# Hash attention and a PReLU feed-forward block on one core: w_out's groups moved to GpSimd's DMA queue and a block later, one step of each weight piece moved behind a reciprocal, second-product weights asked for sooner

## Chip, cores and metric

The kernel runs on one core of a Trainium2 chip. The metric is device time in microseconds (us) of one execution; a kernel's time is the median over its runs. The core has TensorE (PE, matrix products), VectorE (DVE), ScalarE (ACT), GpSimd (POOL) and SyncE (SP), which here only issues DMAs. Each of SP, ACT and POOL has a DMA queue of its own: what an engine issues goes out in the engine's program order, and an issue that has to wait holds up every later one on that engine.

## What is computed

Cut from the reference:

```python
# q, k, v: (4, 8, 768, 64); proj: (64, 6)
q_bucket = sum((q @ proj > 0) * 2 ** arange(6)); k_bucket likewise
scores = where(q_bucket == k_bucket, q @ k.T / 8, -1e9)
attn_out = softmax(scores) @ v
x = attn_out.transpose(0, 2, 1, 3).reshape(3072, 512)
# w_in: (512, 2048), w_out: (2048, 512), alpha: (2048,)
h = x @ w_in
g = maximum(h, 0) + alpha * minimum(h, 0)
out = g @ w_out
```

## The kernel before

`fast_path` does the work in float32. (Another path, `general_path`, stands behind a flag computed at run time and is not entered with these inputs.)

**Attention.** There are 16 pairs (batch, two heads) and two query halves of 384, so 32 units u. For each unit PE computes the scores of six key blocks (L729), ACT takes the exponentials (L734), and PE multiplies them with v (`attend`, L762) into one PSUM bank, tag "av", which has one buffer. The row sums come from DVE and from one accumulating DMA on POOL's queue (L743 to L752: `accp` and `accd`), and PE totals them (`totals`, L774). `divide` (from L778) turns the totals into reciprocals and multiplies: a DVE transpose `st` (L792), two small steps and the reciprocal `rr` (L794), four small POOL copies between partition groups (L797, L798), a DVE transpose `dn` (L800), and L803, which reads the bank "av" and writes x. x goes to a DRAM buffer `x_s` (L804).

**Weight pieces.** Beside the attention, the kernel rewrites the 32 pieces (128x512) of w_in and w_out, one piece a unit: load on SP (L567), `weight_abs` on ACT (L580), `weight_parts` on DVE (four steps, L587 to L592; the first, L587, clamps the piece and keeps its maximum), then `weight_sum` (L613, L618). `divide` calls its argument `between` after the POOL copies have been issued and before `dn`; from unit 1 on this is `weight_rest`, that is `weight_sum(u)` and `weight_group(u)`. So DVE has two weight steps to do while POOL copies. Groups of finished pieces are stored to DRAM, as `w_in_s` and `w_out_r`. `keep_in_program_order` (`do`) fixes the order of the compute instructions on each engine as written; DMA issues outside `do` are placed by the scheduler, by when their buffers come free.

**The two products.** After the attention come, for each of four batches, 8 blocks "1" (`ff1`, x times a weight group, names f_0 to f_7) and 7 blocks "2" (`ff2`, names z_1, z_2, z_5, z_6, z_3, z_7, z_4). Each block is a product of 2x2 blocks done with seven block products instead of eight (L849). Its steps in PE's order are 2 (bank b), 5 (c), 6 (a), 3 (c), 7 (a), then step 1 of the next block (bank a), then step 4 (a). The banks b and c have one buffer each. DVE combines the parts: for f blocks `finish` (L891, L895) four times, and after the "21" part four differences (L899). I call these finish 11, 12, 22 and 21. For z blocks DVE also makes sums of weights (`ws`, L959) and of g (`gs`, L967) for the next block. Between these, DVE runs `sum_out(n)` (L941, four operations 128x256) for the groups n = 0 to 7 of w_out: it takes a group loaded from `w_out_r` (L934), forms sums in place, and the result is stored to `w_out_s` (L942).

**Buffers and loads around the change.** The weight group of an f block, `wi`, is 896 KB with two buffers: `load_w(j + 2)` (L828) can go only when block j's last matmul has read its group. The tag "wl" has two buffers too, and serves w_out's groups (`wo`: tiles of two groups, so wo0, wo2, wo4, wo6) and then the second product's weights (`wl`, 1024 KB, L923). `load_out(n + 3)` follows each odd `sum_out(n)`. All these DMAs are on SP's queue. In SP's order before the change they alternate: wo0, wo2, store 0, wi2, store 1, wi3, wo4, wi4, and so on. `largest` and `verdict` (in block 4) compute the flag on DVE, with four transposes on PE (L1051).

Of the kernel before, what the change touches and what calls it, by code (L numbers as in the profile page):

```python
# [12 lines left out]
ALU = mybir.AluOpType  # L13
# [393 lines left out]
def fast_path(  # L407
# [12 lines left out]
    nc = tc.nc  # L420
# [18 lines left out]
    HI_MIN = 2.0 ** -15  # L439
    HI_END = 2.0  # L440

    do = tc.keep_in_program_order
    PE, DVE, ACT, POOL = nc.tensor, nc.vector, nc.scalar, nc.gpsimd
# [24 lines left out]
    NI = NF // 2  # L468
    NM = 7
    w_in_s = dram.tile([NI, P, NM, 2, P], F32, name="w_in_s")  # L470
    w_out_r = dram.tile([4, P, NI, DM // 2], F32, name="w_out_r")
    w_out_s = dram.tile([4, P, NI, DM // 2], F32, name="w_out_s")
# [90 lines left out]
    def load_weight(i):  # L563
        if i < NW:
            i = order[i]
            raw[i] = pool.tile([P, 512], moe_w_in.dtype, name=f"raw{i}", tag="raw", bufs=3)
            nc.sync.dma_start(raw[i], piece(i))  # L567
# [8 lines left out]
    def weight_abs(i):  # L576
        i = order[i]
        lo, hi = halves(i)
        wx[i] = pool.tile([P, 512], F32, name=f"wx{i}", tag="wx")
        do(ACT.activation(wx[i], hi.bitcast(F32), AF.Abs))  # L580

    def weight_parts(i):
        i = order[i]
        lo, hi = halves(i)
        x = wx[i]
        wr[i] = r = pool.tile([P, 512], F32, name=f"wr{i}", tag="wr", bufs=1)
        do(DVE.tensor_scalar(x, x, HI_MIN, None, op0=ALU.max, op1=ALU.max, accum_out=wmax[:, i : i + 1]))  # L587
        do(DVE.tensor_scalar(
            x.bitcast(U32), x.bitcast(U32), 3, 0xC0000000, op0=ALU.logical_shift_left, op1=ALU.bitwise_xor,
        ))  # L590
        do(DVE.tensor_scalar(r.bitcast(U32), x.bitcast(U32), 0x7F800000, None, op0=ALU.bitwise_and))
        do(DVE.scalar_tensor_tensor(r, lo, 2.0 ** -52, r, op0=ALU.mult, op1=ALU.mult))  # L592
# [31 lines left out]
    def weight_group(i):  # L624

        i = order[i]
        if i >= HW:
            n, m = divmod(i - HW, 2)
            if m == 1:
                nc.sync.dma_start(w_out_r[:, :, n].rearrange("m p d -> p m d"), wst[HW + n])  # L630
            return
        n, m = divmod(i, 4)
        if m < 3:
            return
        w = wst[n]

        def one(to, a, op, c):
            do(DVE.tensor_tensor(w[:, to], w[:, a], w[:, c], op=op))

        def store():  # L640
            c, kk = divmod(n, 2)
            for ii in range(4):
                nc.sync.dma_start(w_in_s[4 * c + ii][:, :, kk], w[:, :, ii])


        for x in ((3, 5, 2), (5, 0, 5), (4, 3, 0), (6, 1, 4)):
            sums_due.append((one, (x[0], x[1], ALU.subtract, x[2])))
        sums_due.append((store, ()))
# [129 lines left out]
    def divide(u, between=lambda: None):  # L778

        pi, g = divmod(u, NCH)
        b, hp = pairs[pi]
        if g == 0:
            vsum[pi] = pool.tile([P, 1], F32, name=f"vs{pi}", tag="vs")
            do(DVE.tensor_scalar(vsum[pi], av[u][:, CW : CW + 1], EPS, None, op0=ALU.mult))
        n = HW2 // 32
        a = pool.tile([P, HW2], F32, name=f"st{u}", tag="st", bufs=1)
        r = pool.tile([P, n], F32, name=f"rc{u}", tag="rc")
        rr = pool.tile([P, 2, n], F32, name=f"rr{u}", tag="rr")  # L790
        d = pool.tile([P, CW], F32, name=f"dn{u}", tag="dn", bufs=1)
        do(DVE.transpose(a, sums[u]))  # L792
        do(DVE.tensor_scalar(r, a.rearrange("p (n w) -> p n w", w=32)[:, :, 0], S * EPS, None, op0=ALU.add))
        do(DVE.reciprocal(rr, r.unsqueeze(1).to_broadcast([P, 2, n])))  # L794
        for q0 in (0, D):
            q1 = q0 + 32
            do(POOL.tensor_copy(rr[q0 : q0 + 32, 1], rr[q1 : q1 + 32, 1]))  # L797
            do(POOL.tensor_copy(rr[q1 : q1 + 32, 0], rr[q0 : q0 + 32, 0]))  # L798
        between()
        do(DVE.transpose(d, rr.rearrange("p h n -> p (h n)").unsqueeze(2).to_broadcast([P, 2 * n, 32])))  # L800

        x = mid.tile([P, CW], F32, name=f"x{u}", tag="x")
        do(DVE.scalar_tensor_tensor(x, av[u][:, :CW], vsum[pi], d, op0=ALU.add, op1=ALU.mult))  # L803
        nc.sync.dma_start(x_s[b, hp][:, g * CW : (g + 1) * CW], x)  # L804
# [124 lines left out]
    def load_out(n):  # L929

        if n < NI:
            t = late[0].tile([P, 2, 4, DM // 2], F32, name=f"wo{n}", tag="wl")
            for i in range(2):
                nc.sync.dma_start(t[:, i], w_out_r[:, :, n + i].rearrange("m p d -> p m d"))  # L934
                w_o[n + i] = t[:, i]

    def sum_out(n):

        w = w_o[n]
        for to, x, op, y in ((2, 3, ALU.add, 2), (3, 0, ALU.subtract, 3), (0, 2, ALU.subtract, 0), (1, 1, ALU.subtract, 0)):  # L940
            do(DVE.tensor_tensor(w[:, to], w[:, x], w[:, y], op=op))  # L941
        nc.sync.dma_start(w_out_s[:, :, n].rearrange("m p d -> p m d"), w)  # L942
        if n % 2:
            load_out(n + 3)

# [143 lines left out]
    add_first(0)  # L1089
    hash_bits(0, second)  # L1090
    weight_abs(0)
    weight_parts(0)
    weight_sum(0)
    for name in "qk":
# [2 lines left out]
    for u in range(UNITS):  # L1097
        pi, g = divmod(u, NCH)

        def weight_rest():  # L1100
            weight_sum(u)
            weight_group(u)

        scores(u, 1)
        if u < last:
            scores(u + 1, 0)
        if u:
            divide(u - 1, weight_rest)
        load_weight(u + 3)
        add_last(u)  # L1110
        add_total(u)
        if u < last:
            add_first(u + 1)
        else:
            now = ff1(0, 0)
            now.step(1)
            now.step(5)
        if g == 0 and pi + 1 < NPAIR:
            hash_bits(pi + 1)
        if g == 1 and pi + 2 < NPAIR:  # L1120
            turn(pi + 2, "q")
            turn(pi + 2, "k")
        if u < last:
            weight_parts(u + 1)
        weight_sums(1)
        attend(u)
        totals(u)
        if u == last:
            divide(u)
        if g == 1 and pi + 2 < NPAIR:  # L1130
            load(pi + 2, "v")
        if u == HW + 2:
            load_w(0)
            load_w(1)
            load_x(0)
        if HW + 4 <= u < HW + 8:
            sum_x(0, u - HW - 4, DVE)
        if u + 2 < NW:
            weight_abs(u + 2)
        if u == 1:  # L1140
            setup_alpha()
        if g == 1:
            for name in "qk":
                magnitude(pi, name)
                if pi + 3 < NPAIR:
                    load(pi + 3, name)
# [10 lines left out]
    for j, (b, what, n) in enumerate(blocks):  # L1157
        n2 = n + 1 if what == "2" else 0 if n == NI - 1 else 7
        if n2 == 0:
            sides_g(b, 0)  # L1160
            sum_w2(b, 0, 3, 4)
        now.step(2) if j else now.step(6)
        if j == 0:
            now.step(3)
            now.step(7)
            now.step(2)
        now.step(22)
        if j == 4:
            largest()
        if 0 < n2 < 7:  # L1170
            sides_g(b, n2)
            sum_w2(b, n2, 3, 4)
        if n2 < 7:
            sum_g2(b, n2, 3, 4)
        if j:
            now.step(5)
            now.step(6)
            now.step(3)
            sum_w2(b, n2, 6)
            now.step(7)  # L1180
            sum_w2(b, n2, 5)
            sum_g2(b, n2, 5)
        if j == 4:
            verdict()
        for n_out in [(0,), (1,), (2,), (3, 4), (5,), (6,), (7,)][j] if j < 7 else ():
            sum_out(n_out)
        if what == "1":
            load_w(b * NI + n + 2)
            if n >= NI - 2:
                load_w2(b, n - NI + 2)  # L1190
        else:
            load_w2(b, n + 2)
            if b + 1 < B:
                if n == 0:
                    load_x(b + 1)
                if n == 6:
                    for m in range(4):
                        sum_x(b + 1, m, DVE)
        if j + 1 < len(blocks):
            turn_out()  # L1200
        else:
            turn_last(0)
        before = now
        if j + 1 < len(blocks):
            b1, what1, n1 = blocks[j + 1]
            now = ff1(b1, n1) if what1 == "1" else ff2(b1, n1)
            now.step(1)
        before.step(4)
        if n2 < 7:
            sum_g2(b, n2, 6)  # L1210
# [29 lines left out]
```

## Time and profile before

| | |
|---|---|
| median of 6 runs | 910.84 us (908.12 to 912.0) |
| the profiled execution, whole time | 913.6 us |
| its span, first to last instruction | 911.8 us |
| mean granted TensorE clock | 0.995 |
| busy: PE / DVE / ACT / POOL | 890.0 / 757.4 / 408.6 / 88.3 us |
| attention and first f_0 steps | 0 to about 353 us |
| first f blocks (f_0 to f_7) | about 353 to 430 us |
| bytes moved | 146.88 MB, mean 161 GB/s |
| transfers on POOL's queue (q0) | 12.58 MB, all of them accp |

The profile is of one execution. "Busy" is the time in which an engine had an instruction in work; PE's busy time says nothing of how well it is used, but its idle time is time in which no matmul ran. A list of waits names, for each group of instructions, whom it waited for, how long in all, how many times, and the longest. A timeline line has start, duration, engine, line of the kernel, operation, what is written from what is read, the shapes, and, in square brackets, the idle time before it and what ended it. "SPq" and "POOLq" are the issues of DMAs on the engines' queues; "to landing" is the time from issue until the data is there.

### The profile page before, as it was taken

What the parts mean: (1) busy time and instruction counts of PE and PEld (TensorE: products, weight loads), DVE (VectorE), ACT (ScalarE), POOL (GpSimd) and SP (SyncE); (2) the same over time, 40 slices, a digit from 0 to 9 for tenths busy, and PEclk for the clock granted to TensorE, in tenths of its full rate; (3) what the DMA queues carried; (4) which work ended last, traced back from release to release, by engine and by line L of the source; (5) the groups of instructions that cost most, each with busy time, mean ns of one, the idle gap of its engine ahead of it and who ended that gap; (6) DMA issues with size and microseconds to landing.
All of it is one profiled execution on the core that took longest, in us unless ns stands there. A gap on an engine that the chain in (4) does not pass through costs nothing.

```text
span 911.8 us, 15639 instructions
## 1 busy us (share of the span) xinstructions
PE 890.0 (98%) x5885; PEld 591.5 (65%) x5885; DVE 757.4 (83%) x1353; ACT 408.6 (45%) x733; POOL 88.3 (10%) x178
## 2 busy tenths in 40 slices
PE   8999999999999999899999999999999999999996
PEld 4444454444444445556998556998556998556996
DVE  4888988988998997798989677989768989768985
ACT  7888888877878873222111222111222111222111
POOL 1222222222223221000000000000000000000000
PEclk9999999999999999999999999999999999999998
DMA  8787887699688764667433535333525242521242
GB/s 225 190 199 163 214 227 187 171 262 244 164 209 204 181 176 150 207 226 246 176 116 110 160 117 162 122 120 109 171 105 174 109 139 88 177 99 40 93 142 70
DMA packets 138053, 146.88 MB, mean 161 GB/s; under 512 B 78304, under 2 KB 126192, under 8 KB 134384
## 3 DMA queue, kind: packets, MB, share of 16 engines
q1 hardware_dynamic: 127248, 132.42, 46.9%
q0 software_dynamic: 8704, 12.58, 8.5%
q8 instruction: 48, 0.79, 0.4%
q10 hardware_dynamic: 2016, 0.79, 0.3%
q14 instruction: 37, 0.30, 0.1%
HBM read 104.87 MB, written 28.31 MB: 146 GB/s over the span
## 4 chain that ended last, share of the span: by engine, by line
PE 56%; DMA 3%; DVE 2%; SPq 1%; issue 1%; POOL 0%; ACT 0%; ACTq 0%; DVEq 0%; POOLq 0%
DMA wi<-w_in_s 3%; PE f_2a L849 2%; PE f_7a L849 2%; PE z_3a L849 2%; PE z_6a L849 2%; PE z_1a L849 2%; PE z_2a L849 2%; PE z_7a L849 2%; PE z_5a L849 2%; PE z_4a L849 2%; PE f_3a L849 2%; PE f_6a L849 2%; PE f_5a L849 2%; PE f_4a L849 2%; PE f_1a L849 2%; PE f_0a L849 2%
## 5 line engine op out<-in xcount | busy, mean ns | idle before, releaser
L734 ACT ACTIVATE pt<-sc 128x768 f32<-128x768 f32 x192 | 152.7, 813 | 53.9 <-PE sc L729 51.3
L729 PE MATMUL sc<-qT,kT 64*128 64x384 f32 x768 | 155.3, 482 | 0.0
L762 PE MATMUL av<-pt,vn 128*32 128x384 f32 (+1 forms) x1536 | 130.6, 488 | 4.9 <-DVE x L803 4.8
L762 PEld LDWEIGHTS av<-pt,vn 128*32 128x32 f32 x1536 | 46.6, 109 | 80.9 <-issue 66.1
L729 PEld LDWEIGHTS sc<-qT,kT 64*128 64x128 f32 x768 | 68.2, 188 | 35.0 <-issue 34.8
L899 DVE TENSOR_TENSOR g<-g,g 128x384 f32<-128x384 f32 x128 | 68.4, 555 | 2.2
L729 PE MATMUL sc<-qb,kb 64*128 64x384 bf16 x384 | 63.4, 324 | 1.9 <-ACT kb L717 1.0
L744 POOL DMA_DIRECT2D accp<-pt x32 | 38.5, 1204 | 193.8 <-issue 93.4
L967 DVE TENSOR_TENSOR gs<-g,gs 128x768 f32<-128x768 f32 x56 | 53.4, 953 | 1.0
L959 DVE TENSOR_TENSOR ws<-wl 128x512 f32<-128x512 f32 x56 | 38.6, 689 | 18.2 <-DMA wl<-w_out_s 15.9
L967 DVE TENSOR_TENSOR gs<-g 128x768 f32<-128x768 f32 x56 | 53.4, 953 | 0.0
L895 DVE SCALAR_TENSOR_TENSOR g<-h,alpha 128x384 f32<-128x384 f32 x32 | 19.8, 617 | 30.3 <-ACT h L888 30.3
L729 PEld LDWEIGHTS <-kb 64*128 64x128 bf16 x384 | 19.4, 94 | 33.2 <-issue 11.1
L752 DVE TENSOR_TENSOR accd<-accd,accp 128x768 f32<-128x768 f32 x32 | 30.7, 958 | 7.7 <-DMA accp<-pt 6.7
L706 ACT ACTIVATE qb<-hs,hb 32x384 bf16<-32x384 f32 x62 | 35.5, 573 | 1.1
L749 DVE TENSOR_TENSOR accd<-accd,pt 128x768 f32<-128x768 f32 x32 | 30.7, 959 | 3.3
L800 DVE STREAM_TRANSPOSE dn<-rr 128x384 f32<-128x384 f32 x32 | 18.5, 579 | 17.4 <-POOL rr L798 17.4
L743 DVE TENSOR_TENSOR accp<-pt,pt 128x768 f32<-128x768 f32 x32 | 30.5, 952 | 2.6 <-ACT pt L734 2.6
L748 DVE TENSOR_TENSOR accd<-pt,pt 128x768 f32<-128x768 f32 x32 | 30.4, 949 | 0.0
L798 POOL COPY rr<-rr 32x6 f32<-32x6 f32 x64 | 27.6, 431 | 2.6
L979 DVE TENSOR_TENSOR m<-m,m 128x768 f32<-128x768 f32 (+1 forms) x36 | 27.1, 752 | 0.7
L717 ACT ACTIVATE kb<-hs,hb 64x384 bf16<-64x384 f32 (+1 forms) x47 | 27.1, 577 | 0.6
(334 smaller groups left out, 1797.3 us busy)
## 6 DMA issues: line engine op xcount, KB each, us to landing
wi<-w_in_s SPq DMA_DIRECT2D x32, 896.0 KB, 4.8
wl<-w_out_s SPq DMA_DIRECT2D x16, 1024.0 KB, 4.8
accp<-pt POOLq DMA_DIRECT2D x32, 384.0 KB, 5.5
wl<-w_out_r SPq DMA_DIRECT2D x12, 1024.0 KB, 4.9
raw<-in_moe_w_out_dram SPq DMA_DIRECT2D x16, 512.0 KB, 5.1
raw<-in_moe_w_in_dram SPq DMA_DIRECT2D x16, 512.0 KB, 4.4
w_in_s<-wsi SPq DMA_DIRECT2D x16, 448.0 KB, 5.7
vn<-in_v_dram SPq DMA_DIRECT2D x16, 384.0 KB, 5.9
```

What stands on the lines that cost most here:

```text
L706: do(ACT.activation(bits["q", pi][D * s : D * s + 32, cols], ps["q"][c : c + 32, half, :CW], AF.Sign, bias=hb[c : c + 32],))
L729: do(PE.matmul(sc[:, s, :CW], what["k", pi][r, ks], what["q", pi][r, qs], start=first, stop=not first,))
L734: do(ACT.activation(pt[:, :, :CW], sc[:, :, :CW], AF.Exp, scale=SCALE / DOWN))
L743: do(DVE.tensor_tensor(accp[u], p(u, 0), p(u, 1), op=ALU.add))
L744: nc.gpsimd.dma_start(accp[u], p(u, 2), accum_op=ALU.add)
L749: do(DVE.tensor_tensor(accd[u], accd[u], p(u, 5), op=ALU.add))
L752: do(DVE.tensor_tensor(accd[u], accd[u], accp[u], op=ALU.add))
L762: do(PE.matmul(av[u][D * s + t : D * s + t + 32, :w], nat["v", pi][:, s, kc * D + t : kc * D + t + 32], prob[u, kc][:, s, :w], start=(kc = ...
L849: do(PE.matmul(self.ps[bank], self.left(left, k), self.right(right, k), start=start and k == 0, stop=k == self.nk - 1, skip_group_check=no ...
L899: do(DVE.tensor_tensor(new_g(b, to)[:, i], g_m[b, x][:, i], g_m[b, y][:, i], op=ALU.subtract))
L959: do(DVE.tensor_tensor(t, w2[b, n, x], w2[b, n, y], op=op))
L967: do(DVE.tensor_tensor(t, g2[b, n, x], g2[b, n, y], op=ALU.subtract))
```

## The change

Three edits:

1. The clamp (L587) is taken out of `weight_parts` into a function of its own, and is called for piece u + 1 in `weight_rest` of unit u, after `weight_sum` and `weight_group`, that is between the POOL copies and `dn`. For the first two pieces it is called ahead.
2. `load_out` and `sum_out` issue their DMAs on POOL's queue instead of SP's, and the groups are summed a block later: none in block 0, then 0, 1, 2, (3, 4), 5, (6, 7) in blocks 1 to 6; before it was 0, 1, 2, (3, 4), 5, 6, 7 in blocks 0 to 6.
3. For batches 1 to 3, `load_w2(b, 0)` and `load_w2(b, 1)` are called in the f blocks 4 and 5 instead of 6 and 7. For batch 0 the condition is the same as before.

```diff
+    def weight_clamp(i):
+        if i < NW:
+            i = order[i]
+            x = wx[i]
+            do(DVE.tensor_scalar(x, x, HI_MIN, None, op0=ALU.max, op1=ALU.max, accum_out=wmax[:, i : i + 1]))
+
     def weight_parts(i):
...
-        do(DVE.tensor_scalar(x, x, HI_MIN, None, op0=ALU.max, op1=ALU.max, accum_out=wmax[:, i : i + 1]))
...
-                nc.sync.dma_start(t[:, i], w_out_r[:, :, n + i].rearrange("m p d -> p m d"))
+                nc.gpsimd.dma_start(t[:, i], w_out_r[:, :, n + i].rearrange("m p d -> p m d"))
...
-        nc.sync.dma_start(w_out_s[:, :, n].rearrange("m p d -> p m d"), w)
+        nc.gpsimd.dma_start(w_out_s[:, :, n].rearrange("m p d -> p m d"), w)
...
     weight_abs(0)
+    weight_clamp(0)
     weight_parts(0)
...
             weight_sum(u)
             weight_group(u)
+            weight_clamp(u + 1)
...
             divide(u - 1, weight_rest)
+        else:
+            weight_clamp(1)
...
-        for n_out in [(0,), (1,), (2,), (3, 4), (5,), (6,), (7,)][j] if j < 7 else ():
+        for n_out in [(), (0,), (1,), (2,), (3, 4), (5,), (6, 7)][j] if j < 7 else ():
             sum_out(n_out)
         if what == "1":
             load_w(b * NI + n + 2)
-            if n >= NI - 2:
-                load_w2(b, n - NI + 2)
+
+            if 0 <= n - NI + (4 if b else 2) < 2:
+                load_w2(b, n - NI + (4 if b else 2))
```

## Prediction

> **What bounds the kernel now.** The page's first part has TensorE (PE) busy 890.0 us of a span of 911.8, so only 21.8 us can be won without taking matmuls away, and the order of PE's and ScalarE's instructions is the same in both kernels. I therefore read the list of waits for PE first, then PE's timeline around each wait, then the timelines of what released it: VectorE (DVE) and SyncE's DMA queue (SP). In the list (engine, tile and line waited for: us in all, times, longest):
>
> ```profile
> PE av L762 <- DVE x L803: 4.8, 9, 1.2
> PE f_2a L849 <- DMA wi<-w_in_s: 2.5, 2, 2.3
> PE sm L774 <- DVE accd L752: 1.4, 1, 1.4
> ...
> PE f_7a L849 <- DMA wi<-w_in_s: 1.1, 1, 1.1
> ...
> PE f_6a L849 <- DMA wi<-w_in_s: 0.5, 1, 0.5
> ```
>
> Two stages hold them. In the attention, the bank "av" has one buffer, so attend(u) waits until DVE's L803 has read it for unit u-1: nine waits, seven of them after 230 us. At the start of the first product, PE waits for weight groups (wi). The rest are start-up and tail, which the change does not touch. Here is PE's timeline where block 1 passes to block 2, and the windows table over the same time (a stretch, its length, busy us of PE, PE's weight loads, DVE, ScalarE and POOL, then granted clock, DMA share, GB/s):
>
> ```profile
> 366.23 1.45 PE L849 MATMUL f_1a<-x,wi 128*128 128x384 f32 x4
> 370.01 2.21 PE L849 MATMUL f_2a<-x,wi 128*128 128x384 f32 x4 [2.33 <-DMA wi<-w_in_s]
> 372.01 2.54 PE L849 MATMUL f_1a<-x,wi 128*128 128x384 f32 x4
> 374.39 1.45 PE L849 MATMUL f_2b<-x,wi 128*128 128x384 f32 x4
> ...
> 368.00:372.00 4.00, 1.99 (x4) 1.13 (x5) 2.86 (x7) 0.25 (x1) 0.00 (x0) 0.85 0.13 56
> 372.00:376.00 4.00, 4.00 (x10) 2.29 (x9) 0.90 (x2) 0.96 (x2) 0.00 (x0) 0.73 0.54 147
> ```
>
> Undisturbed steps start 1.29 us apart. These three intervals take 374.39 - 366.23 = 8.16 instead of 3.87: 4.29 us lost, of which 370.01 - 367.52 = 2.49 is late data and 1.80 the clock, granted at 0.85 and 0.73. By the same sum the passage to block 6 (407.45 to 412.13) loses 0.81 and to block 7 (417.29 to 422.50) 1.34, both at clock 1.00. Together **6.44 us**. Why the group was late stands in SP's timeline:
>
> ```profile
> 357.29 2.02 SPq L934 DMA_DIRECT2D wo<-w_out_r  x4
> 363.22 0.36 SPq L942 DMA_DIRECT2D w_out_s<-wo  x1
> 363.62 0.50 SPq L828 DMA_DIRECT2D wi<-w_in_s  x1
> ```
>
> The buffer of wi2 was free when block 0's last step ended (359.77 + 1.45 = 361.2), but SP stood at the store of w_out's group 0, which waited for DVE's sums (done 363.1), and those for the loaded group. Later wi6 and wi7 were issued in time (402.41, 412.32) but behind 1 MB each on the same queue (wo, wl) and landed after 7.0 and 7.45 us; alone they take 4.8.
>
> **Part 1, the clamp behind the reciprocal.** Per unit, L587 moves from the weight piece's other steps into the gap in which DVE waits for GpSimd's (POOL's) four copies of rr. Nothing is added. DVE's timeline:
>
> ```profile
> 203.34 0.68 DVE L587 TENSOR_SCALAR_CACHE_REDUCE wx<-wx 128x512 f32<-128x512 f32 x1
> ...
> 206.22 0.23 DVE L794 RECIPROCAL rr<-rc 128x12 f32<-128x12 f32 x1
> 206.37 0.63 DVE L613 SCALAR_TENSOR_TENSOR wr<-wx,wr 128x512 f32<-128x512 f32 x1
> 207.03 0.69 DVE L618 SCALAR_TENSOR_TENSOR wso<-raw,wr 128x512 uint32<-128x512 uint32 x1
> 208.25 0.58 DVE L800 STREAM_TRANSPOSE dn<-rr 128x384 f32<-128x384 f32 x1 [0.53 <-POOL rr L798]
> 208.86 0.62 DVE L803 SCALAR_TENSOR_TENSOR x<-av,vs,dn 128x384 f32<-128x384 f32 x1
> ```
>
> The clamp with its accumulator read takes 203.34 to 204.07, about 0.72. Placed at 207.72 it ends at 208.44: the 0.53 gap is filled and dn slips 0.19. DVE's round shrinks by 0.72 - 0.19 = **0.53 a unit**, worth something only where DVE is late. After 214.1 us DVE waits for nothing but POOL's copies, so the 0.53 add up: 1.06, 1.59, 2.12, 2.65, 3.18 by the waits at 232.5, 243.9, 255.2, 266.6 and 277.3, against waits that add up to 0.28, 0.84, 1.99, 2.55, 3.10. Each is covered, with only 0.1 to spare at three of them; the three after 329 (0.77, 0.49, 0.18) lie eleven units on. The one at 167.8 (0.28) has two units behind DVE's last other wait at 148.8. All 4.8 can go; I take **4.5** for the thin margins. Where PE is not waiting, the slip of 0.19 lies within 1.7 us (attend comes 5.7 after the totals, the chain st to x takes 4.0 with the slip). The clamp now needs ScalarE's L580 of the next piece some 6 us sooner; at 236.5 it ran 5 us before DVE would reach the clamp (242). The 1.4 us wait for accd hangs on an accp transfer that took 10.0 us beside wi0 and wi1; it stays (bounds: 1.4 gained, 1 lost).
>
> **Part 2, w_out's groups on POOL's queue, a block later.** 16 DMAs of 512 KB (eight loads, eight stores) leave SP for POOL, which does nothing else then. What it gains: SP's next six issues are wi2 to wi7, nothing between, each on PE's release. The new costs:
>
> (a) *wi beside the other queue.* wi2 goes at 361.3 and is due 367.52: 6.2 us. The first four wo loads (2 MB, from about 356) now run beside it. Bounds 4.3 (shortest wi landing) and 7.45 (behind 1 MB): a stall of 0 to 1.2. I take 0.6; up to 1.07 us of idle the trace shows no drop of the clock. For blocks 6 and 7 (loads and stores of later groups beside them) 0.4 each of the old 2.15 stays.
>
> (b) *DVE falls behind.* One f block is 6.03 us of DVE (three finishes of 1.12, one of 2.66), a group's sums 1.72, largest plus verdict 1.83, the last block's sums for the second product 6.13; PE's block is 9.03. Now blocks 4 and 6 carry two groups: blocks 4 to 7 need 6.03 x 4 + 1.72 x 5 + 1.83 + 6.13 = 40.7, in 36.1 + 0.43 of PE time; before it was 37.2, in 2.15 more. Counted from block 4's start, with blocks 5, 6, 7 and z_1b starting at 9.5, 18.5, 27.5 and 36.6: DVE ends finish 22 of block 4 at 8.35, the verdict 9.9, two groups 13.35, finish 21 16.0, finish 11 of block 5 17.1 (its bank is due at 18.5), group 5 21.1, two groups in block 6 30.6, finish 21 33.3, ws3 and ws4 34.6, finish 11 35.7, gs3 and gs4 37.6, finish 12's first op 38.1 (bank due 37.9), gs5 41.9, finish 21 44.6, gs6 45.4 (due 44.3). In this trace gs6 ended 438.1 for a step at 439.3: 1.2 to spare. So PE waits 0.2 at z_1c, 0.8 for gs6, and, as z_2's sums follow equally late, 1.1 at z_2c: **2.1**.
>
> (c) *A chain on POOL's queue.* wl of z_1 takes the buffer of groups 4 and 5, so it waits for store 5; store 5 stands behind loads 6 and 7, and these wait for store 3. The trace has no plain transfer from POOL; its nearest rows:
>
> ```profile
> accp<-pt POOLq DMA_DIRECT2D x32, 384.0 KB, 5.5
> ...
> w_out_s<-wo SPq DMA_DIRECT2D x8, 512.0 KB, 6.1
> ```
>
> POOL is held 1.20 us by an accp issue of 256 rows; a wo DMA has 512 rows of 1 KB, so 1.2 to 2.4 (estimate). Counted from block 4's start: sums of 3 done 11.6, stored 18.2; loads 6 and 7 issued by 20.6 to 23; store 5 landed 27.5 to 30; wl0_0 landed 32.5 to 35.5. PE wants it at 34.0. Bounds 0 and 1.5; I take 0.5, near the middle of what (b) does not already hide.
>
> The row that shows DVE and POOL in each other's way is POOL's copy of rr: 0.44 and 0.69 us beside DVE's two-input ops, 0.18 when DVE is idle (after 354). An accp issue beside the L591 op at 204 keeps its 1.20, and 1.33 is the longest of 32.
> The Trainium skill (SBUF — State Buffer, SBUF: two separate sides) speaks against this part: it says that a DMA issued from GpSimd starves for descriptors while DVE runs an op in a two-port mode, 0.62 us becoming 3.1. By that factor of five an issue would take 6 us (estimate), and the sum would be that of the slow rival below; by the rows it would be the sum that I give.
>
> Net of part 2: 6.44 - 0.6 - 0.8 - 2.1 - 0.5 = **2.4**.
>
> **Part 3, w2 loads sooner.** For batch 0 the condition is the old one. For later batches the calls move two blocks up, but in the built order of SP's queue the loads stand where they stood (wl1_0 ahead of out's, wl1_1 behind wi11), since SP's order follows when buffers come free. And PE waits for no wl anywhere. Zero; the 0.2 at f_2a in batch 3 stays.
>
> **Sum.** 913.6 (the profiled execution; span 911.8 and 1.8 around it) - 4.5 - 2.4 = 906.7. The median of the six runs shown is 910.84, 2.8 under the profiled one, so 910.84 - 6.9 = **903.9**. About 0.3% (2.7 us) can be told from no change: faster means under 908.1, slower over 913.6.
>
> **Rivals.**
> *All clear* (0.18): wi lands in time beside POOL's transfers and DVE's lag stays within its slack: 4.8 + 6.4 gives 899.6, with the accp wait gone 898.2. For it: wi has 6.2 us for 4.8. Against it: the count of DVE's work.
> *The queue moves, the engines don't* (0.17): the same 16 DMA engines carry both queues; the windows around 364 show a DMA share of 1.07 at 375 GB/s. If wi6, wi7 and z_1's wl are as late as before, part 2 gives -1 to 1 and the time is 905.3 to 907.3.
> *The clamp's gain fails* (0.08): POOL's copies, slowed by one more DVE op, end later, dn slips 0.72 and DVE's round stays: only 2.4, 908.4.
> *Slower: POOL's chain* (0.10). Transfers from POOL land after 10 us, as accp did at 204. Then store 3 lands 22, loads 6 and 7 go until 27.6, store 5 lands 40, wl0_0 at 45 against 34: PE stands 11 us, and 1.8 of slow clock. Part 2 is 6.44 - 1.4 - 12.8 = -7.8, with part 1 +3.3: 914.1. It decides when three such transfers in a row take more than about 9 us. Against it: 7.4 and 10.0 occurred only beside wi0 and wi1; the median is 5.5.
> The forecast keeps 0.47, its own range 901.5 to 906.5.
>
> **Numbers.** Faster: 0.47 + 0.18 + 0.15 of the second = 0.80; same: 0.08 + 0.02 + 0.03 of the last = 0.13; slower 0.07. The range from 899.0 to 909.0 leaves out the slow rival and the far end of the first.
>
> **What would show it.** Part 1: "av <- x" under 1 us in PE's waits, dn's wait for rr near zero. Part 2: f_2a's wait under 1.2 and no clock under 1.00 there; new PE waits on gs or a bank in z_1c, z_1a, z_2c (some 2 us); wl0_0's issue at most 2 us behind block 7's start. Part 3: f_2a late in batch 3 as before. I am wrong if POOL's issues take over 3 us, or if PE waits for wl.

## The result and the profile after

The changed kernel takes **904.14 us** (median of 20 runs, 902.88 to 906.77) against 909.23 for the kernel before (median of 46 runs, 905.15 to 912.98): ratio 0.9947, 95% interval 0.9936 to 0.9957, so some 4.8 us (5.1 by the medians). The forecast was 903.9. The profiled execution took 904.22, close to its kernel's median; that of before, 913.6, lies 4.4 over its own. This difference turns out to matter.

After the change, lines behind L592 stand five further on (L849 is L854, L803 is L808); the clamp is L586. PE's list of waits in the changed kernel (us in all, times, longest):

```profile
PE f_2a L854 <- DMA wi<-w_in_s: 1.7, 1, 1.7
...
PE f_7a L854 <- DMA wi<-w_in_s: 0.9, 1, 0.9
PE f_5a L854 <- DMA wi<-w_in_s: 0.8, 1, 0.8
...
PE z_2a L854 <- DMA wl<-w_out_r: 0.3, 1, 0.3
```

"av <- x" (4.8) and "sm <- accd" (1.4) are gone. The waits for wi have mostly moved: 4.1 us before at f_2, f_6 and f_7, now 3.4 at f_2, f_5 and f_7, with a new one for wl. DVE's timeline of the unit that the prediction showed, now with the clamp in the gap:

```profile
203.85 0.23 DVE L799 RECIPROCAL rr<-rc 128x12 f32<-128x12 f32 x1
203.99 0.63 DVE L618 SCALAR_TENSOR_TENSOR wr<-wx,wr 128x512 f32<-128x512 f32 x1
204.66 0.69 DVE L623 SCALAR_TENSOR_TENSOR wso<-raw,wr 128x512 uint32<-128x512 uint32 x1
205.26 0.68 DVE L586 TENSOR_SCALAR_CACHE_REDUCE wx<-wx 128x512 f32<-128x512 f32 x1
205.87 0.08 DVE L586 DVE_READ_ACCUMULATOR wx<-wx 128x1 f32 x1
205.88 0.58 DVE L805 STREAM_TRANSPOSE dn<-rr 128x384 f32<-128x384 f32 x1
```

From the reciprocal to dn it is 205.88 - 203.85 = 2.03 us, and before the change it was 208.25 - 206.22 = 2.03 as well: dn does not slip at all, and the idle 0.53 is gone. The clamp starts 0.60 us after the op ahead of it, whose recorded duration is 0.69, and dn starts 0.62 after the clamp; L588, which reads the clamp's output, had started 0.73 after it. Over the kernel, dn's wait for POOL falls from 17.4 us (32 times) to 1.5 (twice). PE's timeline and the windows table (its last three columns are granted clock, DMA share, GB/s) where block 1 passes to block 2:

```profile
358.62 1.45 PE L854 MATMUL f_1a<-x,wi 128*128 128x384 f32 x4
361.80 1.56 PE L854 MATMUL f_2a<-x,wi 128*128 128x384 f32 x4 [1.72 <-DMA wi<-w_in_s]
363.19 1.45 PE L854 MATMUL f_1a<-x,wi 128*128 128x384 f32 x4
```

```profile
361.00:363.00 2.00, 1.20 (x4) 0.81 (x5) 1.90 (x5) 0.00 (x0) 0.00 (x0) 1.00 0.01 4
363.00:365.00 2.00, 2.00 (x8) 1.20 (x7) 0.57 (x2) 0.80 (x2) 0.76 (x1) 1.00 0.00 0
```

PE is idle for 1.72 us, as against 2.33, and the clock stays at 1.00. wi2 was asked for at 353.65, nothing in front of it on SP, and landed 8.1 us later; I had 6.2 us for it, and bounds of 4.3 and 7.45. The list of DMAs for these microseconds has (count, size, us to landing):

```profile
wi<-w_in_s SPq DMA_DIRECT2D x1, 896.0 KB, 8.1
```

POOL's queue, over the same stretch:

```profile
349.59 3.06 POOL L939 DMA_DIRECT2D wo<-w_out_r  x4 [2.00 <-issue]
363.90 0.76 POOL L947 DMA_DIRECT2D w_out_s<-wo  x1 [11.25 <-DVE wo L946]
374.92 0.76 POOL L947 DMA_DIRECT2D w_out_s<-wo  x1 [10.26 <-DVE wo L946]
380.16 1.50 POOL L939 DMA_DIRECT2D wo<-w_out_r  x2 [4.48 <-DMA w_out_s<-wo]
383.95 0.76 POOL L947 DMA_DIRECT2D w_out_s<-wo  x1 [2.28 <-DVE wo L946]
```

An issue costs POOL 0.75 to 0.77 us each (four in 3.06), also beside a busy DVE, and these DMAs land after 5.8 and 5.9 us (medians). So POOL itself is no obstacle; what the four loads from 349.59 do is run beside wi2: of the time that packets took between 353.5 and 362 us, their queue has about two thirds.

For the comparison of stages I use two numbers per profile. *Attention*: from the first attend to the second f_0a step. *Lost*: what f_1b to z_5b takes over seven f blocks of 9.03 and two z blocks of 9.10, 81.41 us. Both are read from single executions. The flag's four transposes (0.43 us), which every kernel has, count as lost.

| kernel | profiled run | median | attention | lost |
|---|---|---|---|---|
| before | 913.6 | 909.23 | 331.89 | 7.3 |
| changed | 904.22 | 904.14 | 324.53 | 5.6 |

### The profile page after: what moved, and what is told of

Its sections match the earlier page's. It is cut to its first block, busy times and chain, and to the rows that moved or that the text cites. A ratio compares the mean times of both kernels' runs of the same rounds, so it can differ in the third digit from the quotient of the medians.

```text
span 902.3 us, 15654 instructions
## 1 busy us (share of the span) xinstructions
PE 886.9 (98%) x5885; PEld 590.6 (65%) x5885; DVE 755.0 (84%) x1353; ACT 408.8 (45%) x733; POOL 100.4 (11%) x194
## 4 chain that ended last, share of the span: by engine, by line
PE 93%; DMA 3%; DVE 1%; SPq 0%; issue 0%; ACT 0%; ACTq 0%
PE sc L734 17%; PE av L767 14%; PE z_2a L854 2%; PE f_0a L854 2%; PE f_2a L854 2%; PE f_5a L854 2%; PE z_4a L854 2%; PE z_6a L854 2%; PE z_3a L854 2%; PE z_7a L854 2%; PE z_5a L854 2%; PE f_3a L854 2%; PE f_6a L854 2%; PE f_4a L854 2%; PE f_1a L854 2%; PE z_1a L854 2%
## 5 line engine op out<-in xcount | busy, mean ns | idle before, releaser
L734 PEld LDWEIGHTS <-kb 64*128 64x128 bf16 x384 | 19.4, 94 | 33.4 <-issue 11.3
L748 DVE TENSOR_TENSOR accp<-pt,pt 128x768 f32<-128x768 f32 x32 | 30.5, 952 | 2.5 <-ACT pt L739 2.5
L803 POOL COPY rr<-rr 32x6 f32<-32x6 f32 x64 | 27.6, 431 | 2.6
L802 POOL COPY rr<-rr 32x6 f32<-32x6 f32 x64 | 19.8, 310 | 64.7 <-DVE rr L799 63.4
```

Of the source, the lines that this page charges most:

```text
L734: do(PE.matmul(sc[:, s, :CW], what["k", pi][r, ks], what["q", pi][r, qs], start=first, stop=not first,))
L748: do(DVE.tensor_tensor(accp[u], p(u, 0), p(u, 1), op=ALU.add))
```

## Experiments

**One part at a time.** First the clamp alone (L587 becomes `weight_clamp(u + 1)` in `weight_rest`, the rest as before).

> Only the clamp is moved; w_out's groups stay on SP's queue in their old blocks. If the parts add up and the clamp's share is the list's waits "av <- x" (4.8 us): 4 to 5 us under the kernel before, no "av <- x" wait left in PE's list, f_2a still late by 1.5 to 2.5 us. Rival A: the profiled execution of before (4.4 us over its median) had more of these waits than a usual one; then only 2 to 3.5 us under. Rival B: POOL's four copies end later by as much as the clamp takes, and dn slips by the whole 0.72; then under 2.5 us and "av <- x" waits of over 1 us remain.

Measured: 904.33 us (6 runs), ratio 0.9944 (0.9922 to 0.9965), which is 5.1 us. Attention 324.53, no "av <- x" in the list. All of the change's gain is here. One part of the expectation missed: f_2a was 2.9 us late, not 1.5 to 2.5.

Then w_out's groups alone:

```diff
-                nc.sync.dma_start(t[:, i], w_out_r[...])
+                nc.gpsimd.dma_start(t[:, i], w_out_r[...])
-        nc.sync.dma_start(w_out_s[...], w)
+        nc.gpsimd.dma_start(w_out_s[...], w)
-        for n_out in [(0,), (1,), (2,), (3, 4), (5,), (6,), (7,)][j] if j < 7 else ():
+        for n_out in [(), (0,), (1,), (2,), (3, 4), (5,), (6, 7)][j] if j < 7 else ():
```

> w_out's groups on POOL's queue and a block later; the clamp stays where it was before. If the parts add up: 1 to 2.5 us under the kernel before, with "av <- x" at 4 to 5 us in PE's waits and f_2a late by 1.7, f_5a 0.8, f_7a 0.9 us, as in the changed kernel. Rival A (the profiled execution of before lost more at f_2 than a usual one): 0 to 0.7 us under. Rival B (the parts help each other only together): over before, or 4 us and more under.

Measured: 910.03 us (12 runs), ratio 1.0002 (0.9989 to 1.0016): nothing gained, although its profile loses only 5.1 where that of before loses 7.3. f_2a, f_5a and f_7a were late by less than expected (1.1, 0.5 and 0.8 us), but z_2a waited 1.1 us for wl. Rival A comes nearest. The queue alone (the first four diff lines, without the last two):

> Only the queue is changed: w_out's groups on POOL's queue, summed in the old blocks 0 to 6; the clamp as before. If what counts is that wi2 no longer stands behind store 0 on SP's queue: as the kernel with queue and block changed, 1 to 2.5 us under before, and f_2a late by 1.5 to 2 us since the four early wo loads are beside it as well. Rival: without the later block DVE's sums stand as before and no block carries two groups but block 3, so DVE lags less and it is 0.5 to 1 us better still. Other rival: store 0's data now crosses wi2's on the 16 DMA engines, f_2a is late by over 2.3 us, and it is within 0.5 us of before.

Measured: 909.76 us, ratio 1.0006 (0.9991 to 1.0021). Lost in its profile: 7.0, no better than before, though wi2 no longer stands behind a store. PE's waits for wi:

```profile
PE f_6a L849 <- DMA wi<-w_in_s: 1.8, 1, 1.8
PE f_2a L849 <- DMA wi<-w_in_s: 1.6, 1, 1.6
PE f_7a L849 <- DMA wi<-w_in_s: 1.5, 1, 1.5
```

The last rival comes nearest in time, although f_2a is late by 1.6 us and not by 2.3: what was a wait in the queue is now a slow transfer (wi2 lands after 8.0 us). The loads of part 3 alone (the `load_w2` condition):

> Only the second product's loads are called two blocks sooner in batches 1 to 3. The instructions of every engine stand in the same order as before. Expected: no difference, within 0.5 us of before, and the profile shows what varies from one execution of this program to the next: how late f_2a is, whether the clock falls there, and whether PE waits for accd. Rival (the call's place changes the waits of the loads): 1 us or more either way.

Measured: 909.74 us, ratio 1.0002 (0.9990 to 1.0014). Nothing, as expected; and no "sm <- accd" wait; no other profile has one either, so the 1.4 us of it before belonged to that one execution.

**What the profile of before showed by chance.** The kernels before and with the clamp alone were profiled a second time.

> The kernel before, unchanged, for a second profile of it. If profiled executions of kernels in which store 0 stands ahead of wi2 lose more at f_2 than usual ones do (three of three so far lie 2.2 to 4.4 us over their medians): 910.5 to 913, with 4 to 5 us lost between f_1b and f_2b and a granted clock under 1.00 there. If the first profile was just a bad one: 907 to 910, with f_2a late by under 2 us and no fall of the clock. The 1.4 us wait for accd is not there again in either case, as it was not in the kernel with the loads alone moved.

> The kernel with the clamp alone moved, unchanged, for a second profile. If profiled executions of kernels with store 0 ahead of wi2 are the long ones: 906 to 908 and 4 to 5 us lost between f_1b and f_2b. If not: 902 to 904.5 and under 3 us lost there. PE's list has no "av <- x" in either case.

Measured: 910.6 and 905.75 us (the second just under the expected 906 to 908); lost 6.4 and 7.6. So far five profiles of five with store 0 ahead of wi2 lose 4.2 to 4.8 us between f_1b and f_2b alone. Here is the second one of the kernel before, PE's timeline and the windows:

```profile
363.04 1.45 PE L849 MATMUL f_1a<-x,wi 128*128 128x384 f32 x4
366.76 2.93 PE L849 MATMUL f_2a<-x,wi 128*128 128x384 f32 x4 [2.27 <-DMA wi<-w_in_s]
369.48 1.77 PE L849 MATMUL f_1a<-x,wi 128*128 128x384 f32 x4
```

```profile
366.00:368.00 2.00, 1.24 (x2) 0.84 (x3) 1.90 (x5) 0.00 (x0) 0.00 (x0) 0.68 0.01 4
368.00:370.00 2.00, 2.00 (x4) 1.01 (x3) 0.02 (x1) 0.27 (x1) 0.00 (x0) 0.50 0.52 180
370.00:372.00 2.00, 2.00 (x7) 1.15 (x6) 0.20 (x1) 0.68 (x2) 0.00 (x0) 0.97 0.24 82
```

An idle of 2.27 us, and then a clock of 0.50: steps of 1.29 us take 2.72 and 1.61 (start to start). If the clock is either 1.00 or 0.50, the three windows hold 1.28, 2.00 and 0.12 us at 0.50, 3.4 us in all (an estimate from these lines). But the next experiment's kernel has the same order of DMAs, and its profile does not show this:

```profile
361.05 1.45 PE L854 MATMUL f_1a<-x,wi 128*128 128x384 f32 x4
364.32 1.56 PE L854 MATMUL f_2a<-x,wi 128*128 128x384 f32 x4 [1.81 <-DMA wi<-w_in_s]
365.71 1.45 PE L854 MATMUL f_1a<-x,wi 128*128 128x384 f32 x4
```

Idle 1.81, clock 1.00 in the two windows after it, lost 4.8 in all, less than in the changed kernel. So the stall at f_2 stands close to a threshold that lies somewhere between 1.81 and 2.27 us in these profiles. The mean clock, which every run reports, hints at how often an execution is beyond it: the five profiles with the fall report 0.995 or 0.996, the nine others 0.997 to 0.999. Of 62 runs of the kernel before in these comparisons 17 have 0.998 or more (median 907.85), 19 have 0.996 or less (median 910.65), and the 26 at 0.997 tell nothing. The changed kernel isn't free of it, as far as this goes: 4 of its 20 runs have 0.996 or less, and these are its four slowest (905.64 to 906.77).

**Is it the gap?** The clamp out of `weight_parts`, but behind L803 instead of ahead of dn:

```diff
             divide(u - 1, weight_rest)
+        weight_clamp(u + 1)
```

> The kernel before, with the clamp taken out of weight_parts and put behind L803 (after x is written), not into the gap ahead of dn. The DVE work of a unit is the same and the gap of 0.53 us stays idle. If the gain is the filled gap: nothing gained, 908.5 to 910, and "av <- x" waits of 4 to 5 us in PE's list. Rival: it is enough that the clamp is no longer ahead of st in its round; then the waits go here too, and it is 904 to 905.

Measured: 907.59 us (12 runs), ratio 0.9977 (0.9962 to 0.9992): 2.1 us, between the two forecasts. Attention 326.59; "av <- x" is down to 1.6 us. The gap is still idle, so the gap is not all of it. DVE's timeline of this kernel:

```profile
249.85 0.58 DVE L805 STREAM_TRANSPOSE dn<-rr 128x384 f32<-128x384 f32 x1 [0.53 <-POOL rr L803]
250.46 0.62 DVE L808 SCALAR_TENSOR_TENSOR x<-av,vs,dn 128x384 f32<-128x384 f32 x1
250.99 0.68 DVE L586 TENSOR_SCALAR_CACHE_REDUCE wx<-wx 128x512 f32<-128x512 f32 x1
251.60 0.08 DVE L586 DVE_READ_ACCUMULATOR wx<-wx 128x1 f32 x1
251.60 0.95 DVE L753 TENSOR_TENSOR accd<-pt,pt 128x768 f32<-128x768 f32 x1
```

The clamp now takes 0.61 until accd starts; ahead of L588 it took 0.72, since L588 reads what the clamp wrote and started 0.12 after the accumulator's read, while accd does not depend on it and starts with that read. DVE's x in three ordinary units, first before, then here:

```profile
297.00 0.62 DVE L803 SCALAR_TENSOR_TENSOR x<-av,vs,dn 128x384 f32<-128x384 f32 x1
307.51 0.62 DVE L803 SCALAR_TENSOR_TENSOR x<-av,vs,dn 128x384 f32<-128x384 f32 x1
317.96 0.62 DVE L803 SCALAR_TENSOR_TENSOR x<-av,vs,dn 128x384 f32<-128x384 f32 x1
```

```profile
292.49 0.62 DVE L808 SCALAR_TENSOR_TENSOR x<-av,vs,dn 128x384 f32<-128x384 f32 x1
302.87 0.62 DVE L808 SCALAR_TENSOR_TENSOR x<-av,vs,dn 128x384 f32<-128x384 f32 x1
313.18 0.62 DVE L808 SCALAR_TENSOR_TENSOR x<-av,vs,dn 128x384 f32<-128x384 f32 x1
```

From one x to the next, ordinary units took DVE 10.44 to 10.51 us before, 10.31 to 10.38 here; PE's own round is 10.42 (attend to attend, 20.84 for two). That is the explanation of the half success: DVE's round was just over PE's, so whatever a unit with extra DVE work (11.3, the sums of x and of w_in) ran late was never made up. With 0.13 less a unit DVE catches up a little; in the gap the clamp takes 0.72 off each round, and the same extra units take 10.59 to 10.65.

**What is left of the loss.** wi2 gets space of its own (in tiles that are first used in the second product) and is asked for before the wo loads, once in the changed kernel, once in the kernel with the clamp alone.

```diff
+            if n == 2:
+                w_m[n] = {}
+                for m, tag in ((0, "m1"), (3, "m5"), (6, "o")):
+                    t = late[0].tile([P, 3, 2, P], F32, name=f"wi2_{m}", tag=tag, bufs=2 if tag == "o" else 1)
...
+    load_w(2)
     load_out(0)
     load_out(2)
```

> The changed kernel, but wi2 of batch 0 has space of its own (three tiles that are first used in the second product) and is asked for before the wo loads; so wi2 waits for no release and wi3 to wi7 are asked for a block sooner. If what is left in the f blocks is the short time between a release of wi's two buffers and the next need of a group: the 4.7 us that the changed kernel loses from f_1b to z_1b go. Then either DVE's lag, which these stalls covered, comes up in the z blocks (2 us and more, where the changed kernel loses 0.85): 901 to 902; or it does not: 899 to 900. Rival: the transfers slow each other whatever the buffers are, and the stalls move to f_3 and f_4: 903 and over.

> The kernel with the clamp alone moved (w_out's groups on SP's queue in their old blocks), and wi2 with space of its own, asked for before the wo loads. If the loss in the f blocks is the release of wi's buffers and the store ahead of wi2, and not the queue: PE loses nothing from f_1b to z_1b, 898.5 to 900.5, and it is at least as good as the same with POOL's queue, since no block carries two groups late. Rival: the 7 us lost there in its profiled execution are not in its usual runs; then it gains under 2 us, 902.5 to 904.5. Other rival: stores and loads of groups ahead of wi on one queue keep f_5 to f_7 late: 902 to 903 with the waits in the profile.

Measured: 901.33 us, ratio 0.9920 (0.9893 to 0.9947), lost 3.1; and **900.39**, ratio 0.9904 (0.9879 to 0.9929), lost 2.3. (One thing in the first expectation was wrong: only wi2, wi3 and wi4 come sooner. wi5 takes the buffer of wi3 and has as little time as ever. So its time, 901 to 902, was met for another reason: the waits at f_5a and f_7a stay, and z_1 and z_2 lose 0.8, not 2 and more.) PE's waits in the two, first with POOL's queue, then with SP's:

```profile
PE f_7a L864 <- DMA wi<-w_in_s: 1.0, 1, 1.0
PE z_2a L864 <- DMA wl<-w_out_r: 0.4, 1, 0.4
...
PE f_5a L864 <- DMA wi<-w_in_s: 0.3, 1, 0.3
```

```profile
PE vd L1066 <- DVE top L1059: 0.9, 1, 0.9
```

With SP's queue the waits for wi are gone, the old blocks of the groups notwithstanding: of the three wi asked for between 388 and 412 us the median lands after 5.3 us, and beside POOL's transfers after 7.4. What comes up in their place is DVE: PE waits 0.9 us at the verdict's transposes, in block 4, behind the block with two groups. The second forecast, that PE loses nothing from f_1b to z_1b, was met in time but not there: PE loses 1.95 us, 0.43 of it the four transposes themselves. The own space for wi2 ends the wait for it at f_2 (f_1b to f_2b takes 9.03 us with POOL's queue, 9.32 with SP's), and in these two profiles there is no fall of the clock.

The later block on SP's queue, clamp moved, no own space:

> The clamp moved and w_out's groups a block later, but on SP's queue as before. In SP's order wi2 and wi3 now stand ahead of store 0. If the later block alone takes the store out of wi2's way: as the changed kernel, 903 to 905, with f_2a late by under 2 us. If POOL's transfers beside wi cost the changed kernel something: 1 to 2 us better than it, 902 to 903. If the queue is what counts (stores and loads that wait for DVE hold later wi issues on SP): f_5 to f_7 late by 3 us and more in all, 905 to 907.

Measured: 903.22 us, ratio 0.9934 (0.9909 to 0.9959). By time it isn't told apart from the changed kernel; its profile loses 4.7 against 5.6. Up to the end of the first batch these two differ in the queue alone (the calls of part 3 touch the later batches), and the start of the f stage shows what that does: wi2 is asked for at 353.89 here and lands after 7.0 us, behind the wo loads on one queue, and f_2a is 0.62 late; beside them on two queues it takes 8.1 and f_2a is 1.72 late.

```profile
wi<-w_in_s SPq DMA_DIRECT2D x1, 896.0 KB, 7.0
```

Two limits to this. It is one profile against four: beside 2 MB on POOL's queue wi2 took 8.1, 8.1, 8.0 and, in the kernel with the groups alone, 7.5 us. And POOL takes 3.06 us to issue the four loads where SP takes 2.02, so the last of them goes out later; no run separates this from the sharing. Another wait matters here: PE waits 0.7 us for DVE at z_2c, where I had expected DVE's lag.

Groups in pairs in blocks 1 and 2, not 4 and 6, in the changed kernel (`[(), (0, 1), (2, 3), (4,), (5,), (6,), (7,)]`):

> The changed kernel with w_out's groups summed as (0, 1), (2, 3), 4, 5, 6, 7 in blocks 1 to 6, so that no late block carries two groups. If the loss of 0.85 us in the z blocks and of z_2a is DVE's lag and POOL's chain: it goes, and 0.5 to 1.5 us are gained, 902.7 to 903.7. Rival: loads and stores come sooner beside wi3 and wi4 and make f_3 to f_5 later by as much: 904 to 905, with new waits on wi.

Measured: 904.08 us, ratio 0.9964 (0.9939 to 0.9989), from 902.52 to 911.14. The profile (902.52) has no wait at z_2a or f_7a and a new one of 0.6 at f_4a, lost 3.7. But four of eleven runs took 907.9 to 911.1; why, no profile shows. This stays open.

Last, in the best kernel, `largest` in block 2 instead of 4:

> The kernel with the clamp moved, groups on SP's queue in their old blocks, and wi2 in space of its own; and the three reductions of largest are done in block 2, not 4, where PE waited 0.9 us for them. If that wait is DVE's lag, uncovered since the stalls on wi are gone: 0.5 to 0.9 us better than without this edit, 899.5 to 900, no vd wait. Rival: the lag only moves to the next bank or group: 900.4 as before, with a new PE wait on DVE of 0.5 us or more.

Measured: 901.08 us, ratio 0.9909 (0.9892 to 0.9926): no gain over 900.39. The rival is right, the lag only moves, to two places with 0.7 us together:

```profile
PE vd L1066 <- DVE f_4p L906: 0.4, 1, 0.4
PE f_5b L864 <- DVE row L1067: 0.3, 1, 0.3
```

| kernel | profiled run | median | attention | lost |
|---|---|---|---|---|
| before, second profile | 910.6 | 909.23 | 329.15 | 6.4 |
| loads only | 911.89 | 909.74 | 329.57 | 7.5 |
| groups only | 909.85 | 910.03 | 330.50 | 5.1 |
| queue only | 910.51 | 909.76 | 329.01 | 7.0 |
| clamp behind x | 907.03 | 907.59 | 326.59 | 4.8 |
| clamp only, twice | 907.12, 905.75 | 904.33 | 324.53, 324.53 | 7.5, 7.6 |
| clamp, later block, SP | 903.21 | 903.22 | 324.53 | 4.7 |
| own space, SP's queue | 900.07 | 900.39 | 324.53 | 2.3 |

All eight profiles with the clamp in the gap have an attention of 324.52 or 324.53 us: PE no longer waits for DVE there, and the spread goes as well.

## Why the forecast came out right, and where its steps did not

**The total** hit because two errors cancel, which is luck: 903.9 against 904.14. Six runs gave a median of 910.84 for the kernel before, 46 give 909.23, so the base was 1.6 us too high; and I forecast 6.9 us of gain where 4.8 to 5.1 came, 1.8 to 2.1 too much.

**Part 1** had the right mechanism and was sized too small. I took 4.5; the clamp alone gives 5.1 (3.2 to 7.1), in the profiles 324.53 against 329.0 to 331.9. The term that was off: "0.53 us a unit saved, dn slips 0.19". dn does not slip: I had laid the recorded durations end to end (0.69 for the op ahead, 0.72 for the clamp, 1.41 in all), but the clamp starts 0.60 after the op ahead and dn 0.62 after the clamp, 0.19 less. So the round shrinks by 0.72: some 0.2 more a unit, so after five or six units there is about 1 us to spare where I had counted 0.1. I also named the gap as the sole source; the clamp behind x shows that 0.13 a unit elsewhere already gives 2.1 of the 5.1, because DVE's round (10.44 to 10.51) lay so close to PE's (10.42).

**Part 2** failed as a sum: "Net of part 2: 6.44 - 0.6 - 0.8 - 2.1 - 0.5 = 2.4", measured 0 (1.0 gained to 1.5 lost), and 0.2 with the clamp moved as well (904.33 to 904.14).
- The 6.44 was read from one execution, 2.8 us over its median, and then taken off the median in full. The 1.80 of clock and part of the late data at f_2 seem to come in some executions only; where they do not (the profile with the clamp behind x) the old order loses 4.8, less than the changed kernel. In runs with a mean clock of 0.998 or more the medians are 907.85 before and 908.85 with the groups alone (17 and 7 runs).
- (a) was too small: 1.4 us of waits for wi forecast, 3.4 found. wi2 took 8.1 us, above the upper bound that I had from a wi behind 1 MB (7.45): at its issue 2 MB had been asked for on the other queue only 4.1 us and less before. The Trainium skill (DMA: Bandwidth & Descriptors, Issuing engines are not separate DMA queues) says that transfers from all issuers run on the same 16 engines and interleave, and that a second issuer saves issue time alone; the 7.5 to 8.1 us against 7.0 on one queue agree, and go further, since here the urgent transfer beside the second queue came later.
- (b) was too large: 2.1 forecast, and with (c) 2.6; the z blocks z_1 and z_2 lose 0.9, of which 0.35 is the wait for wl. The error is that of (a) seen from the other side: PE's additional waits give DVE time. Counted from block 4's start (382.54), the last two groups' sums were done at 30.5 and 31.7 us, where I had 30.6 for both, but PE started z_1b at 38.8 and not at 36.6. That DVE's work is nearly as tight as I counted shows where the waits for wi shrink or go: 0.7 us at z_2c with the later block on SP's queue, 0.9 at the verdict with own space.
- (c) was about right (0.5 taken, 0.35 at z_2a; 1.1 with the groups alone and 0.4 with own space, within the bounds of 0 and 1.5). By my own sign, "if PE waits for wl", I was wrong, though the wait is small; that sign did not fit a sum that had 0.5 for it. The issue price of 1.2 to 2.4 us was really 0.75. No issue shows anything of the factor of five that I had weighed from the Trainium skill (SBUF — State Buffer, SBUF: two separate sides). A later section of that page, Who interferes with whom, says that tensor_tensor, most of DVE's work in these blocks, has no two-port mode; the 0.75 us agree with that.
- Of my rivals, "the queue moves, the engines don't" described part 2 (-1 to 1). Its total of 905.3 to 907.3 was off because part 1 gave more and the base was lower.

**Part 3**: zero, as forecast (1.0002, 0.9990 to 1.0014). I had said that batch 3's 0.2 at f_2a stays; it is gone from the profile of the changed kernel, from that of the loads alone, and also from those of the clamp and of the groups alone. So it goes without the loads too; what it hangs on, the runs do not show.

Of the signs that I named, "av <- x" and dn's wait came true, the clock at 1.00 in the profile too (four other runs may not have it), and wl0_0 was issued at 411.12, ahead of f_7b (412.31). f_2a's wait did not (1.7, not under 1.2), and some 2 us of PE waits on gs and banks in z_1 and z_2 did not appear.

**Open**: the runs do not tell whether the later block on SP's queue is worth anything by time (903.22 and 904.33, intervals overlapping), what makes single executions fall on one side or the other at f_2, or why four runs with the groups in pairs took 4 us and more longer.

## What to carry to other kernels

A stall read from one profile may be taken off a median only if it is in the usual execution: compare the profile's time with the median first, and take a second profile where they differ by as much as the gain in question. Compare the rounds of two coupled engines before counting the waits between them; where they differ by under 1%, a tenth of a microsecond per round decides about several. Moving bulk transfers to another queue frees the urgent one from waiting behind them, but not from sharing the engines with them; a buffer that lets the urgent load start a block sooner did more than either queue (904.33 to 900.39 us on SP's queue, 904.14 to 901.33 on POOL's; the queues by themselves 904.33 and 904.14).

## What the runs showed of the hardware

- PE idle for 1.72 and 1.81 us left the granted clock at 1.00; idle for 2.27 to 2.89 us (five profiles) came with 3.4 us at 0.50, by the sum shown above, in each of the five. The Trainium skill (TensorE: Matmul & The Clock Gate, Part 1: The HAM clock gate) gives an idle window of about 3.4 us as what brings the half rate: the half rate agrees, but 2.27 us were enough here, and the measurement decides.
- At f_2, a wi load of 896 KB landed after 5.9 to 7.5 us behind a store of 512 KB on one queue (six profiles), 7.0 behind 2 MB on the same queue (one) and 7.5 to 8.1 beside 2 MB on POOL's (four).
- A DVE op with an accumulator lets an independent op start with its accumulator read (0.61 us from its start), a dependent one 0.11 to 0.12 us later. An op without one is alike: one with a recorded duration of 0.69 us (L623) let the next, independent op start 0.60 us after its own start.
